# One more folded piece, of 16 rows, at the end of pass one, and other DMA times in the planner of pass two

## The chip, the cores and the metric

The kernel runs on one core of a Trainium2 chip. The metric is the device time of the whole program in microseconds, from several runs; beside it stands one execution taken by the hardware profiler. The engines are called PE (matrix), DVE (vector), ACT (scalar), POOL and SP (here it only issues the DMAs of rows).

## The reference

The input `x` is 1 x 384 x 384 x 384 in bfloat16, the weight `w1d` one number (k = 1, so the padding is empty):

```python
g = jnp.einsum("bhwc->bc", x) / (H * W)
s = jnp.zeros_like(g)
for i in range(k):
    s = s + gp[:, i:i + C] * w1d[i]
s = _sigmoid(s)
return x * s[:, None, None, :]
```

So each channel's mean over all 147,456 positions is needed before the first output can be written. `x` has 113 MB and does not fit on chip; it is read once for the mean, and what was not kept is read a second time for the product.

## The kernel before

**Rows.** The positions are dealt to 128 partitions, 1152 to each. A "row" below is one position in every partition: 384 channels, 768 B a partition, 98,304 B in all. A chunk of n rows in one DMA is a run of n x 768 B in each partition. The tile `arena` holds `ROWS` rows; all loads, scales and stores work in it.

**Pass one** sums the rows: every row that lands is multiplied on PE with a matrix of ones (`sum_rows`, L253, one matmul a row, all into one PSUM bank). Rows of the first chunk (`STREAMED`, 785 rows) are summed and overwritten; rows of the second (`KEPT`, 367 rows) stay. To keep more rows than there is room for, groups of rows are **folded** (`fold`, L292): of a piece of p = 4 rows times four (16 rows), the exponent bits that all values share are taken out, so that the fourth row of each four is hidden in bits of the other three; 16 rows then take 12. `GROUPS` lists the groups: the first piece (16 rows), eight pairs of pieces (32 rows each) in two columns, and `BANKED`, whose folded rows are parked in PSUM. A fold is 10 instructions on DVE and 2 tests on ACT (L313) that check that the bits are as assumed; it uses 16 scratch rows, T (8 rows) and Y (8 rows). The loop at L416 takes each group (`take`), folds it and streams other rows meanwhile through the room not used yet (`BETWEEN`, `SLOTS` of 13 rows from A). At the end `take_raw` (L433) fills all that is left, the scratch last, with kept rows that are not folded: U, V (8 rows each), the 39 rows from A, Y and T. The seam follows: last matmul, sigmoid into `s_bf` (L443), a copy of it in PSUM (L447).

**Order in pass one.** All row DMAs are issued by SP in the order of the program, and each first waits for the last reader of the rows it overwrites (PE's sum, DVE's or ACT's last use). So a load that waits holds back all loads behind it.

**Pass two** scales and stores the kept rows, unfolds the groups (`unfold`, L470: DVE steps `fields`, `three`, `fourth`, which rebuild and scale three quarters and then the last quarter of a piece), and reads the 785 streamed rows again through whatever room has come free, scales and stores them. POOL scales three pieces of 4 rows beside DVE. The order of SP's and DVE's instructions is not written by hand: a **planner** (L564 to L767) steps a clock in 0.05 us, with a cost per row (`ROW`), per load and store, a latency before a transfer moves (`LAT`) and until its end is seen (`SEEN`), and emits each load, scale, unfold step and store when its model says that it is due. `needed` holds the scratch rows that must be stored before a column of groups may be unfolded, `home` and `free` say which column a group uses, `order` in which order the groups come. The planner fixes the order alone; on the chip each instruction still waits for its semaphores.

Of the kernel before, what the change touches and what calls it, by code (L numbers as in the profile page):

```python
# [127 lines left out]
def kernel(  # L128
# [25 lines left out]
    PIECE = 4  # L154
    PAIR = 2 * PIECE
    PAIRS = 4
    U = 3 * PIECE + PAIRS * 3 * PAIR
    G0 = U + PAIR
    V = G0 + PAIRS * 3 * PAIR
    A = V + PAIR  # L160
    N_A = 39
    T = A + N_A
    Y = T + 2 * PIECE
    ROWS = Y + 2 * PIECE
# [3 lines left out]
    GROUPS = [(0, PIECE)]  # L168
# [4 lines left out]
            GROUPS.append((a + 3 * PAIR * i, PAIR))  # L173
    BANKED = len(GROUPS)
    GROUPS.append((A, 6))
    PS = 3 * GROUPS[BANKED][1]
    N_RAW = ROWS - V + PAIR
    pool = ctx.enter_context(tc.tile_pool(name="sb", bufs=1))
    psum = ctx.enter_context(tc.tile_pool(name="psum", bufs=1, space=bass.MemoryType.PSUM))

# [24 lines left out]
    def rows(lo, n):  # L205
        return [("a", r) for r in range(lo, lo + n)]
# [5 lines left out]
    N_STREAM = RPP - N_RAW - sum(4 * q for _, q in GROUPS)  # L212
    N_KEPT = RPP - N_STREAM
    assert N_STREAM % 2 and N_KEPT % 2
    STREAMED, KEPT = (0, N_STREAM), (N_STREAM, N_KEPT)
    r = 0
    c_group = []
# [3 lines left out]
    c_raw = r  # L221
    assert r + N_RAW == N_KEPT

    def raw(a):

        return c_raw + (a - U if a < G0 else PAIR + a - V)


    summed = [0]
# [43 lines left out]
    def bits(dst, src, op0, s0, op1, s1, reads, writes):  # L273
        fl.add(
            "DVE",
            lambda: nc.vector.tensor_scalar(out=dst, in0=src, scalar1=s0, scalar2=s1, op0=op0, op1=op1),  # L276
            reads=reads, writes=writes,
        )

    def join(dst, a, b, op, reads, writes):  # L280
        fl.add(
            "DVE", lambda: nc.vector.tensor_tensor(out=dst, in0=a, in1=b, op=op), reads=reads, writes=writes  # L282
        )

    def flat(a, p):
        return arena[:, a : a + p, :].bitcast(u16)

    SHL, SHR, AND, OR, XOR = (
        Op.logical_shift_left, Op.logical_shift_right, Op.bitwise_and, Op.bitwise_or, Op.bitwise_xor,
    )  # L290
# [56 lines left out]
    streamed = [0]  # L347
# [10 lines left out]
    def stream_all(where, n=None):  # L358
        i = 0
        n = sum(m for _, m in where) if n is None else n  # L360
        while n:
            a, m = where[i % len(where)]
            m = min(n, m)
            stream(m, a)
            n -= m
            i += 1

    def take(g, lo=0, hi=None):

        a, q = GROUPS[g]  # L370
        hi = 4 * q if hi is None else hi
        load(KEPT, a + lo, c_group[g] + lo, c_group[g] + hi)
        sum_rows(a + lo, hi - lo)

    def of_group(g):
        return [i for i, piece in enumerate(pieces) if piece[0] == g]
# [12 lines left out]
    for i, bk in enumerate(banks):  # L389
# [4 lines left out]
    S1, S2, S3 = ([slot] for slot in SLOTS)  # L394
# [8 lines left out]
    BETWEEN = [  # L403
        LOW_COLUMN, HIGH,
        LOW_COLUMN, [(A, 39)],
        [(G0 - 24, 24), (A - 24, 24)], (S1, S2 + S3),
        (S1, S2 + S3 + S1), (S2, S3 + S1),
    ]
    between = sum(n for b in BETWEEN for w in b for _, n in (w if isinstance(w, list) else [w]))
    first = N_STREAM - between  # L410
    stream_all(EARLY[3:], first % 48)
    stream_all(EARLY, first - first % 48)
# [3 lines left out]
    for g, where in zip(range(1, BANKED), BETWEEN):  # L416
# [6 lines left out]
        else:  # L423
# [4 lines left out]
            take(g, 12, 24)  # L428
            fold(k2)
            stream_all(where[1])  # L430
    assert streamed[0] == N_STREAM

    def take_raw(a, n):  # L433
        load(KEPT, a, raw(a), raw(a) + n)
        sum_rows(a, n)

    for a, n in S2 + [(U, 8)] + S3 + S1 + [(V, 8), (Y + 2, 6), (T + 6, 4), (T + 3, 3), (T + 1, 2), (T, 1)]:
        take_raw(a, n)
    assert summed[0] == RPP

# [29 lines left out]
    def unfold(k, first):  # L470

        g, lo, p = pieces[k]
        a, at = first + 3 * lo, first + 3 * GROUPS[g][1] + lo
        w, wc = flat(a, 3 * p), [rows(a + j * p, p) for j in range(3)]
        w0, w1, w2 = (flat(a + j * p, p) for j in range(3))
        ba, ca = Y, Y + PIECE
        u, b, c = flat(at, p), flat(ba, p), flat(ca, p)
        uc, bc, cc = rows(at, p), rows(ba, p), rows(ca, p)

        def fields():  # L480
            bits(u, w0, SHR, 4, AND, 0x0780, wc[0], uc)
            bits(b, w1, SHR, 8, AND, 0x0078, wc[1], bc)
            bits(c, w2, SHR, 12, AND, 0x0007, wc[2], cc)
            join(u, u, b, OR, uc + bc, uc)
            bits(b, w2, SHL, 4, AND, 0x8000, wc[2], bc)
            join(u, u, c, OR, uc + cc, uc)

        def three():
            wall = wc[0] + wc[1] + wc[2]
            bits(w, w, AND, 0x87FF, OR, 0x3800, wall, wall)  # L490
            join(u, u, b, OR, uc + bc, uc)
            scale(a, 3 * p)

        def fourth():

            bits(u, u, XOR, FIX, AND, 0xFFFF, uc, uc)
            scale(at, p)

        return [
            (fields, 4 * TS(p) + 2 * TT(p)),  # L500
            (three, TS(3 * p) + TT(p) + TT(3 * p)),
            (fourth, TS(p) + TT(p)),
        ]

    def TS(n):
        return 0.15 + 0.1 * n

    def TT(n):
        return 0.15 + 0.2 * n
# [51 lines left out]
    written = []  # L561


    ROW, PER_LOAD, PER_STORE = 0.2267, 0.112, 0.061  # L564
    LAT, SEEN, DT = 2.0, 1.5, 0.05
    PENDING, MERGE = 24.0, 12.0
    BIG, CAP, PART, LOW, LAST = 32, 48, 16, 9.0, 4.0
    DEEP, SHORT = 6.5, 1.0
# [26 lines left out]
    def send(chunk, a, lo, hi, then, known=None):  # L595

        waiting.append((dve_at, hi - lo, then, chunk, a, lo, [] if known is None else known))
# [8 lines left out]


    SCRATCH = rows(Y, 8)
    needed = [set(SCRATCH + rows(U, 8)), set(SCRATCH + rows(V, 8)), set(SCRATCH)]

    def stored(a, n):

        def f():
            for i in range(a, a + n):
                for left in needed:
                    left.discard(("a", i))
                if not Y <= i < Y + 8 and not U <= i < U + 8 and not V <= i < V + 8:
                    idle[i] = True
        return f


    for a, n in (
        (Y, 4), (Y + 4, 4), (T, 4), (T + 4, 4), (A + 26, 6), (A + 32, 7), (A + 13, 13), (V + 4, 4), (A, 13)
    ):
        landed.append((KEPT, a, raw(a), n, True))

# [2 lines left out]
    t = 1.0  # L629
# [3 lines left out]
        alongside.append((t, KEPT, a, raw(a), n))  # L633


    order = [g for i in (3, 2) for g in (1 + 2 * i, 2 + 2 * i)] + [BANKED]
    order += [g for i in (1, 0) for g in (1 + 2 * i, 2 + 2 * i)] + [FIRST]
    line = deque(order)
    home = {g: i for i, column in enumerate(COLUMNS) for g in column}
    home[BANKED] = 2  # L640
    free = [True, True, True]
    total = len(GROUPS)
    out_rows = 0
    turns = deque()
# [5 lines left out]
    def start_group():  # L650

        if not line:
            return False
        g = line[0]
        column = home[g]
        if needed[column] or not free[column] or g == BANKED and (bank_at is None or now < bank_at[1]):
            return False
        line.popleft()
        free[column] = False
        a, q = GROUPS[g]  # L660
        if g == BANKED:
            a = bank_at[0]

        below = 0
        if column < 2 and g != COLUMNS[column][0]:
            below = GROUPS[COLUMNS[column][COLUMNS[column].index(g) - 1]][1]

        def part():
            release(a + below, sent - below)

        def done():
            nonlocal out_rows
            out_rows += 1
            free[column] = True
            release(a + max(below, sent), 4 * q - max(below, sent))

        for k in of_group(g):
            fields, three, fourth = unfold(k, a)
            turns.extend((fields + (None,), three + (None,), fourth + (None,)))
        sent = 0  # L680
        if len(line) >= total - N_SPLIT and q == PAIR:

            f, t, _ = turns[-5]
            sent = 3 * PIECE
            turns[-5] = (f, t, lambda: send(KEPT, a, c_group[g], c_group[g] + sent, part, written))
        f, t, _ = turns[-1]
        turns[-1] = (f, t, lambda: send(KEPT, a + sent, c_group[g] + sent, c_group[g] + 4 * q, done, written))
        return True

    while True:  # L690

        if dve_at <= now:
# [4 lines left out]
            if landed and (ahead < PENDING or not can):  # L697
                chunk, a, lo, n, end = landed.popleft()
# [43 lines left out]
        if got and todo < N_STREAM:  # L742
            n, a = max(got)
            n = min(n, CAP, N_STREAM - todo)
            ahead = backlog()

            queue = sum(e[1] for e in moves)
            turn = last_is_load or queue >= DEEP or queue < SHORT
            if turn and (todo or not landed and not waiting) and (n >= BIG or n == N_STREAM - todo or (ahead < LOW and n >= 8) or ahead < LAST):
                last_is_load = True  # L750
                load(STREAMED, a, todo, todo + n)
                for i in range(a, a + n):
                    idle[i] = False
                parts = [(STREAMED, a + e, todo + e, f - e, f == n) for e, f in split(n, PART)]
                todo += n
                moves.append([now + LAT, n * ROW + PER_LOAD, lambda parts=parts: landed.extend(parts)])
# [44 lines left out]
```

## Time and profile before

| what | value |
|---|---|
| median of 3 runs | 720.13 us (719.99 to 720.31) |
| the profiled execution, its own time | 720.71 us |
| its span, first to last instruction | 718.7 us |
| busy: DVE, PE, ACT, POOL | 494.5, 211.0, 115.7, 9.8 us |
| DMA | 303.79 MB, mean 423 GB/s |
| HBM read, written | 190.41 MB, 113.25 MB |
| last matmul of pass one ends, first store is issued | 267.80, 269.42 us |

The span is cut in 40 slices of 18 us in the page's second part; a digit is a unit's busy share in tenths. A row of the chain of waits has a start, a length and what was waited for; start plus length of a DMA row is the moment at which that transfer had landed. In a timeline row stand start, length, engine, line, operation, shapes and count.

### The profile page before, as it was taken

How to read it: one execution, taken by the hardware profiler on the slowest of the kernel's cores; microseconds unless marked ns; L12 is line 12 of the kernel's file. 1: busy time of each engine (PE TensorE's matmuls, PEld its weight loads, DVE VectorE, ACT ScalarE, POOL GpSimd, SP SyncE). 2: the span in 40 equal slices, each digit the busy share in tenths (PEclk: the TensorE clock that was granted, in tenths of full speed). 3: DMA queues.
4: the chain of work that ended last, by engine and by line, in shares of the span. 5: the costliest groups of instructions: out<-in, count | busy, mean ns of one | idle time of the engine just before them, and what ended most of it. 6: DMA issues, size and time to landing. Idle time of an engine off the chain costs nothing.

```text
span 718.7 us, 2062 instructions
## 1 busy us (share of the span) xinstructions
PE 211.0 (29%) x1202; PEld 0.3 (0%) x3; DVE 494.5 (69%) x472; ACT 115.7 (16%) x93; POOL 9.8 (1%) x7
## 2 busy tenths in 40 slices
PE   4678778987887770000000000000000000000000
PEld 0000000000000000000000000000000000000000
DVE  4600003888999719998999999999999865450840
ACT  3600002666677510002000000000000000000000
POOL 0000000000000004000000000000000000000000
PEclk9899999999999995555555555555555555555555
DMA  9999999999999979999999999999999999999997
GB/s 383 428 444 429 427 427 437 436 437 422 427 426 428 428 330 392 405 429 427 428 429 424 431 436 433 431 438 429 437 429 433 428 435 430 439 429 429 434 437 307
DMA packets 20173, 303.79 MB, mean 423 GB/s; under 512 B 2242, under 2 KB 2498, under 8 KB 5570
## 3 DMA queue, kind: packets, MB, share of 16 engines
q1 hardware_dynamic: 20160, 303.67, 99.0%
q8 instruction: 4, 0.07, 0.0%
q14 instruction: 7, 0.06, 0.0%
q10 hardware_dynamic: 2, 0.00, 0.0%
HBM read 190.41 MB, written 113.25 MB: 422 GB/s over the span
## 4 chain that ended last, share of the span: by engine, by line
DMA 72%; DVE 16%; PE 5%; ACT 2%; another core or an unknown queue 1%; SPq 0%; issue 0%; DVEq 0%
DMA arena<-in_x_dram 54%; DMA out_dram<-arena 19%; DVE arena L456 12%; PE bank L242 5%; DVE arena L276 3%; ACT arena L313 2%; DVE arena L282 1%; SPq L236 0%; ACT s_bf L443 0%; SPq L466 0%; DVEq L112 0%; SPq L796 0%; SPq L112 0%; SPq L106 0%
## 5 line engine op out<-in xcount | busy, mean ns | idle before, releaser
L456 DVE TENSOR_TENSOR arena<-arena,s_bf 128x1536 bf16<-128x1536 bf16 (+9 forms) x97 | 229.0, 2390 | 76.0 <-DMA arena<-in_x_dram 60.3
L276 DVE TENSOR_SCALAR arena<-arena 128x1536 uint16<-128x1536 uint16 (+2 forms) x247 | 145.3, 633 | 118.1 <-DMA arena<-in_x_dram 102.1
L242 PE MATMUL bank<-arena,ones 128*128 128x384 bf16 x1151 | 202.5, 336 | 48.2 <-DMA arena<-in_x_dram 48.0
L313 ACT ACTIVATE arena<-arena 128x3072 uint16<-128x3072 uint16 (+1 forms) x38 | 102.5, 2696 | 142.1 <-DVE arena L276 142.1
L282 DVE TENSOR_TENSOR arena<-arena 128x1536 uint16<-128x1536 uint16 (+2 forms) x114 | 121.0, 1061 | 5.0 <-PE bank L242 2.6
L529 PE MATMUL bank<-odd,ones 128*128 128x1 bf16 x1 | 0.2, 187 | 322.7 <-DVE odd L524 322.7
L456 POOL TENSOR_TENSOR arena<-arena,s_bf 128x1536 bf16<-128x1536 bf16 x3 | 9.6, 3238 | 268.4 <-ACT bank L447 268.4
L386 ACT COPY arena<-bank 128x512 uint32<-128x512 uint32 (+1 forms) x7 | 4.0, 571 | 56.2 <-DMA out_dram<-arena 56.0
L456 DVE TENSOR_TENSOR arena<-arena,bank 128x1536 bf16<-128x1536 bf16 (+3 forms) x8 | 11.6, 1520 | 0.0
L242 PE MATMUL bank<-zeros,ones 128*128 128x384 bf16 x48 | 8.3, 326 | 0.0
L313 ACT ACTIVATION_READ_ACCUMULATOR arena<-arena 128x1 f32 x38 | 7.1, 186 | 0.0
L386 ACT COPY bank<-arena 128x512 uint32<-128x512 uint32 (+1 forms) x7 | 3.6, 567 | 0.0
L443 ACT ACTIVATE s_bf<-bank,w_sc 128x384 bf16<-128x384 f32 x1 | 0.6, 581 | 14.2 <-PE bank L242 14.2
L256 PE MATMUL bank<-arena,ones 128*128 128x384 bf16 x1 | 0.5, 478 | 6.7 <-DMA arena<-in_x_dram 6.7
L769 ACT ACT_TABLE_LOAD x1 | 1.3, 1283 | 0.7 <-PEq L785 0.7
L343 DVE TENSOR_SCALAR w_sc<-bank 128x1 f32<-128x1 f32 x1 | 0.2, 159 | 1.1 <-PE bank L338 1.1
L333 DVE MEMSET ones<- 128x128 bf16 x1 | 0.2, 165 | 1.1 <-SPq L106 1.1
L338 PE MATMUL bank<-w_bf,ones 1*128 1x1 bf16 x1 | 0.2, 182 | 2.1 <-DMA w_bf<-in_w1d_dram 2.1
L529 PEld LDWEIGHTS bank<-odd,ones 128*128 128x128 bf16 x1 | 0.1, 105 | 581.4 <-DVE odd L524 581.4
L533 DVE CAST odd_i<-bank 128x1 int32<-128x1 f32 x1 | 0.2, 159 | 0.3 <-PE bank L529 0.3
L447 ACT COPY bank<-s_bf 128x192 uint32<-128x192 uint32 x1 | 0.3, 323 | 0.0
L519 DVE TENSOR_REDUCE worst<-seen 128x1 f32<-128x38 f32 x1 | 0.2, 186 | 0.0
(8 smaller groups left out, 0.9 us busy)
## 6 DMA issues: line engine op xcount, KB each, us to landing
arena<-in_x_dram SPq DMA_DIRECT2D x15, 4608.0 KB, 35.5
arena<-in_x_dram SPq DMA_DIRECT2D x20, 1248.0 KB, 14.2
out_dram<-arena SPq DMA_DIRECT2D x6, 3072.0 KB, 33.0
out_dram<-arena SPq DMA_DIRECT2D x4, 4608.0 KB, 40.2
arena<-in_x_dram SPq DMA_DIRECT2D x5, 3072.0 KB, 22.5
arena<-in_x_dram SPq DMA_DIRECT2D x6, 2304.0 KB, 18.5
out_dram<-arena SPq DMA_DIRECT2D x11, 1248.0 KB, 10.9
arena<-in_x_dram SPq DMA_DIRECT2D x3, 4512.0 KB, 27.2
```

Source lines behind the costliest of these rows:

```text
L242: return pe.add_instruction(mybir.InstMatmult(name=nc.get_next_instruction_name(), ins=[pe.lower_ap(rhs), pe.lower_ap(ones[:])], outs=[pe. ...
L256: return nc.tensor.matmul(acc, lhsT=ones[:], rhs=arena[:, i, :], start=first, stop=last)
L276: lambda: nc.vector.tensor_scalar(out=dst, in0=src, scalar1=s0, scalar2=s1, op0=op0, op1=op1),
L282: "DVE", lambda: nc.vector.tensor_tensor(out=dst, in0=a, in1=b, op=op), reads=reads, writes=writes
L313: lambda: nc.scalar.activation(out=y, in_=y, func=ACTF.Copy, accum_out=seen[:, 2 * k + i : 2 * k + i + 1]),
L333: fl.add("DVE", lambda: nc.vector.memset(ones[:], 1.0), writes=["ones"])
L386: "ACT", lambda: nc.scalar.copy(dst.bitcast(u32), src.bitcast(u32)), reads=reads, writes=writes
L443: lambda: nc.scalar.activation(out=s_bf[:], in_=acc, func=ACTF.Sigmoid, scale=w_sc[:, 0:1]),
L447: "ACT", lambda: nc.scalar.copy(s_ps.bitcast(u32), s_bf[:].bitcast(u32)), reads=["s_bf"], writes=["bank0"]
L456: lambda: vec.tensor_tensor(out=v, in0=v, in1=s[:, None, :].to_broadcast([P, n, C]), op=Op.mult),
L529: lambda: nc.tensor.matmul(votes, lhsT=ones[:], rhs=odd[:], start=True, stop=True),
L769: nc.scalar.preload_act_table(ACTF.Sigmoid)
```

## The change

- A new group `LATE` of one piece (16 rows) lies at A, where slots lay before. It is taken and folded after the eight pairs. Its 12 folded rows stay from A, and `D` = A + 12 names the 4 rows that come free; the rows kept raw go from 71 to 59, so 371 rows are kept instead of 367 and 781 are streamed.
- The slots of the last two pairs and the final raw loads are cut anew: 13, then 16 and 10 rows; 8 streamed rows (`SPARE`) go through U while the new piece is folded.
- In pass two `LATE` is unfolded first, in a home of its own (3), which waits until Y and D are stored.
- `unfold` has four steps instead of three: `fields` is cut in `fields` and `signs`, with the same six instructions in another order.
- The planner's `LAT` goes from 2.0 to 0.4 us.

```diff
+    LATE = len(GROUPS)
+    GROUPS.append((A, PIECE))
+    D = A + 3 * PIECE
     PS = 3 * GROUPS[BANKED][1]
-    N_RAW = ROWS - V + PAIR
+    N_RAW = 2 * PAIR + ROWS - D
...
-        return c_raw + (a - U if a < G0 else PAIR + a - V)
+        return c_raw + (a - U if a < G0 else PAIR + a - V if a < A else 2 * PAIR + a - D)
...
         [(G0 - 24, 24), (A - 24, 24)], (S1, S2 + S3),
-        (S1, S2 + S3 + S1), (S2, S3 + S1),
+        (S1, S2 + S3), ([(A, 16)], [(A + 16, 10)] + S3),
     ]
+    SPARE = [(U, 8)]
...
+    take(LATE)
+    for k in of_group(LATE):
+        fold(k)
+    stream_all(SPARE)
+    assert streamed[0] == N_STREAM
+
-    for a, n in S2 + [(U, 8)] + S3 + S1 + [(V, 8), (Y + 2, 6), (T + 6, 4), (T + 3, 3), (T + 1, 2), (T, 1)]:
+    for a, n in [(D + PIECE, 10)] + S3 + [(V, 8), (U, 8), (D, PIECE), (Y + 2, 6), (T + 6, 4), (T + 3, 3), (T + 1, 2), (T, 1)]:
         take_raw(a, n)
...
             bits(b, w1, SHR, 8, AND, 0x0078, wc[1], bc)
+            join(u, u, b, OR, uc + bc, uc)
+
+        def signs():
             bits(c, w2, SHR, 12, AND, 0x0007, wc[2], cc)
-            join(u, u, b, OR, uc + bc, uc)
             bits(b, w2, SHL, 4, AND, 0x8000, wc[2], bc)
             join(u, u, c, OR, uc + cc, uc)
...
-            (fields, 4 * TS(p) + 2 * TT(p)),
+            (fields, 2 * TS(p) + TT(p)),
+            (signs, 2 * TS(p) + TT(p)),
...
-    LAT, SEEN, DT = 2.0, 1.5, 0.05
+    LAT, SEEN, DT = 0.4, 1.5, 0.05
...
-    needed = [set(SCRATCH + rows(U, 8)), set(SCRATCH + rows(V, 8)), set(SCRATCH)]
+    needed = [set(SCRATCH + rows(U, 8)), set(SCRATCH + rows(V, 8)), set(SCRATCH), set(SCRATCH + rows(D, PIECE))]
...
-        (Y, 4), (Y + 4, 4), (T, 4), (T + 4, 4), (A + 26, 6), (A + 32, 7), (A + 13, 13), (V + 4, 4), (A, 13)
+        (Y, 4), (Y + 4, 4), (D, PIECE), (T, 4), (T + 4, 4), (A + 26, 6), (A + 32, 7), (V + 4, 4), (D + PIECE, 10)
...
-    order = [g for i in (3, 2) for g in (1 + 2 * i, 2 + 2 * i)] + [BANKED]
+    order = [LATE] + [g for i in (3, 2) for g in (1 + 2 * i, 2 + 2 * i)] + [BANKED]
...
-    home[BANKED] = 2
-    free = [True, True, True]
+    home[BANKED], home[LATE] = 2, 3
+    free = [True] * 4
```

More of the change, by code (lines that the diff above doesn't have):

```diff
@@ L406 @@
         [(G0 - 24, 24), (A - 24, 24)], (S1, S2 + S3),
-        (S1, S2 + S3 + S1), (S2, S3 + S1),
+        (S1, S2 + S3), ([(A, 16)], [(A + 16, 10)] + S3),
     ]
-    between = sum(n for b in BETWEEN for w in b for _, n in (w if isinstance(w, list) else [w]))
+    SPARE = [(U, 8)]
+    between = sum(n for b in BETWEEN + [SPARE] for w in b for _, n in (w if isinstance(w, list) else [w]))
     first = N_STREAM - between
@@ L430 @@
             stream_all(where[1])
-    assert streamed[0] == N_STREAM
     def take_raw(a, n):
@@ L608 @@
     SCRATCH = rows(Y, 8)
-    needed = [set(SCRATCH + rows(U, 8)), set(SCRATCH + rows(V, 8)), set(SCRATCH)]
+    needed = [set(SCRATCH + rows(U, 8)), set(SCRATCH + rows(V, 8)), set(SCRATCH), set(SCRATCH + rows(D, PIECE))]
+    FOURTH = set(rows(U, 8) + rows(V, 8) + rows(D, PIECE) + SCRATCH)
     def stored(a, n):
@@ L616, in f @@
                     left.discard(("a", i))
-                if not Y <= i < Y + 8 and not U <= i < U + 8 and not V <= i < V + 8:
+                if ("a", i) not in FOURTH:
                     idle[i] = True
@@ L677, in start_group @@
         for k in of_group(g):
-            fields, three, fourth = unfold(k, a)
-            turns.extend((fields + (None,), three + (None,), fourth + (None,)))
+            turns.extend(step + (None,) for step in unfold(k, a))
         sent = 0
         if len(line) >= total - N_SPLIT and q == PAIR:
-            f, t, _ = turns[-5]
+            f, t, _ = turns[-6]
             sent = 3 * PIECE
-            turns[-5] = (f, t, lambda: send(KEPT, a, c_group[g], c_group[g] + sent, part, written))
+            turns[-6] = (f, t, lambda: send(KEPT, a, c_group[g], c_group[g] + sent, part, written))
         f, t, _ = turns[-1]
```

## The prediction

> **What bounds the kernel now.** I read the slices of the span first, because they show at once which unit is never idle.
>
> ```profile
> DMA  9999999999999979999999999999999999999997
> GB/s 383 428 444 429 427 427 437 436 437 422 427 426 428 428 330 392 405 429 427 428 429 424 431 436 433 431 438 429 437 429 433 428 435 430 439 429 429 434 437 307
> ```
>
> The 16 DMA engines are busy in every slice but the one at the seam of the two passes and the last one, so the time is the number of rows moved times the time of a row, plus the places where the queue is not at full rate. The chain of waits says the same:
>
> ```profile
> DMA 72%; DVE 16%; PE 5%; ACT 2%; another core or an unknown queue 1%; SPq 0%; issue 0%; DVEq 0%
> ```
>
> Then the stretches, to see at which rate and where it dips (columns: engines' busy time, PE clock, DMA share, GB/s).
>
> ```profile
> 64.00:135.00 71.00, 58.85 (x338) 0.00 (x0) 14.80 (x20) 11.43 (x8) 0.00 (x0) 0.95 1.01 435
> 136.00:250.00 114.00, 93.69 (x557) 0.00 (x0) 100.13 (x135) 77.14 (x54) 0.00 (x0) 1.00 1.01 430
> 300.00:420.00 120.00, 0.00 (x0) 0.00 (x0) 113.56 (x96) 4.00 (x7) 0.00 (x0) 0.50 1.01 429
> 260.00:270.00 10.00, 7.08 (x43) 0.00 (x0) 1.57 (x2) 0.90 (x2) 1.17 (x1) 1.00 0.58 234
> 270.00:280.00 10.00, 0.00 (x0) 0.00 (x0) 10.00 (x8) 0.00 (x0) 8.46 (x3) 0.58 1.01 412
> 280.00:290.00 10.00, 0.00 (x0) 0.00 (x0) 9.93 (x12) 0.00 (x0) 0.00 (x0) 0.50 1.03 401
> 290.00:300.00 10.00, 0.00 (x0) 0.00 (x0) 9.97 (x10) 0.00 (x0) 0.00 (x0) 0.50 0.99 386
> ```
>
> A row (128 partitions of 768 B, 98,304 B) costs 98,304 B / 435 GB/s = 0.226 us where transfers are 32 to 48 rows long. Three things lie above that rate: the seam near 267 us, a slow patch from 270 to 300 us, and small transfers (430 and 429 GB/s). DVE is busy 113.56 of 120 us from 300 to 420, so it hides behind the DMA with little room.
>
> **The change part by part.**
>
> 1. *Rows.* The kept rows go from 367 to 371, so the rows read twice go from 785 to 781. Four rows fewer at 0.226 us: **-0.90 us**. All of it is on the bound, the DMA queue.
>
> 2. *Transfers.* I counted SP's list in both kernels: 140 row transfers before (51 in pass one, 89 in pass two), 152 after (52 and 100). Slots of 13 rows became 16 and 10, and pieces of 24 or 32 rows became more and smaller ones. What one more transfer costs inside a full queue comes from two places. In the chain of waits these two landings
>
> ```profile
> 236.84 13.94 DMA arena<-in_x_dram
> 253.13 8.44 DMA arena<-in_x_dram
> ```
>
> are at 250.78 and 261.57, and SP's list has 13, 8, 13 and 13 rows between them: 10.79 us for 47 rows in 4 transfers. 47 x 0.226 is 10.62, so 0.04 us a transfer. The stretch 300 to 420, at 429 instead of 435 GB/s, loses 1.4% of 120 us, 1.7 us, on about 32 transfers: 0.05. I take 0.04, the lower, because it is free of the planner's other waits: 12 x 0.04 = **+0.48 us**; the bounds are 0 and 0.05 (0 to +0.6). SP issues the twelve in 0.34 us each, while it mostly waits.
>
> A store with nothing ahead of it shows what the queue hides:
>
> ```profile
> out_dram<-arena SPq DMA_DIRECT2D x1, 384.0 KB, 2.3
> ```
>
> That is the first store, issued at 269.42; 4 rows carry 0.94 us of that, so 1.4 us are fixed. Such a cost is met only where the queue is empty. The Trainium skill ("DMA: Bandwidth & Descriptors", Measured) says to batch to at least 1 MiB for 75% of peak, and (Anatomy of one DMA) puts a fixed 2.0 us on each; it speaks against this change, whose 10-row pieces are 960 KB. By that rule the twelve transfers would cost 24 us. Here four transfers averaging 1.1 MB took 10.79 us, 428 GB/s, so queued transfers do not show it in this trace.
>
> 3. *One fold more at the end of pass one.* Consecutive folds of one piece start 7.83 us apart:
>
> ```profile
> 219.16 1.90 DVE L276 TENSOR_SCALAR arena<-arena 128x3072 uint16<-128x3072 uint16 x3
> 226.99 1.90 DVE L276 TENSOR_SCALAR arena<-arena 128x3072 uint16<-128x3072 uint16 x3
> 253.47 0.19 ACT L313 ACTIVATION_READ_ACCUMULATOR arena<-arena 128x1 f32 x1
> ```
>
> It costs nothing as long as the loads queued behind it come early enough. Before, the last load landed near 267.2 us (issued near 255.9, 11.4 to landing). Counting back from there over the new list (1, 2, 3, 4, 6 rows, then D 4, U 8, V 8, S3 13, 10, spare 8; 0.226 a row, 0.04 a transfer), the new piece's 16 rows land at 251.7. DVE is free by then: the last pair's first 12 rows arrive some 3 us sooner, since a 13-row load ahead of them is gone and with it the 2.6 us that DVE waited for them at 237; its two folds run from 234.8 to 250.6. So the new fold runs from 251.7 to 259.5. The 6-row load into the scratch waits for the last ACT test, which ended 7.80 us after its fold's start before (253.66 against 245.86): it is issued at 259.6, and the queue has work until 263.4. That is 3.8 us of cover; the first load of the program, 24 rows or 5.4 us landing 7.9 us after issue, shows a start-up of 2.5. **0 us, with 1.3 us to spare**; beyond that each us of a later fold is a us of time. The seam itself (last matmul, sigmoid, first scale, first store) is not edited: 0.
>
> 4. *The opening of pass two.* DVE unfolds the new piece first and stores its 16 rows in one go. Order on the queue: stores of 59 rows in 12 transfers, loads of 21 and 10 rows, then this store. From 270.8 (first data) that is 59 x 0.226 + 0.48 = 13.8 us to 284.6, and 7.1 us more to 291.7. DVE's side: eight scales of 47 rows, 12.47 us before for nine scales of 59 rows less 12 x 0.2 us and one start, so 268.43 to 278.4. Then one unfold, from the pitch of
>
> ```profile
> 280.82 1.49 DVE L276 TENSOR_SCALAR arena<-arena 128x1536 uint16<-128x1536 uint16 x3
> 290.62 1.49 DVE L276 TENSOR_SCALAR arena<-arena 128x1536 uint16<-128x1536 uint16 x3
> ```
>
> 9.8 us, so the store goes out at 288.3: 3.4 us of cover, less 1.4 fixed, **2.0 us to spare** (before, the first unfolded store went out at 289.3 with work until 301.4). The next three stores (10, 11, 10 rows, scales of 2.15, 2.35, 2.15 us after the loads land at 289.4 and 291.7) go out at 291.6, 294.0 and 296.1 and are needed at 295.4, 297.7 and 300.2; then 47 rows of loads need no DVE and the cover grows to some 9 us. I carried the same running sum on, DVE's durations against rows: the thinnest place further on is near 360 us, some 3 us. So 0; the piece adds 6.4 us of conversion to DVE (9.8 less the scales 2.47 and 0.96), hidden by DMA.
>
> 5. *The planner's latency, the split of the unfold into four steps, the fourth home.* They change only the order that is counted in 2 and 4. SP, POOL (its three scales are the same) and ACT get no work on the path: 0.
>
> Sum: -0.90 + 0.48 = -0.42 us. The profiled execution took 720.71 us (span 718.7 and 2.0 around it), so 720.29 by its own measure; it stands 0.58 above the median of the runs, 720.13, and against that the forecast is **719.7 us**. About 0.2%, 1.44 us, is what a measurement of this kernel can tell from no change; this is inside.
>
> **The rivals.**
>
> *The slow patch moves (faster).* From 270 to 300 the rates are 412, 401 and 386 with the DMA share at 0.99 to 1.03: the engines are busy and slow, no wait explains it. Against 430 this is 10 us x (0.042 + 0.067 + 0.102) = 2.1 us. The change replaces just these transfers (13-row stores and loads by 10). If the patch goes, 719.7 - 2.1 = 717.6; half of it, 718.7. For it: the rate is 429 once the order settles. Against: the new opening is the same kind, small stores and then the first loads. It could as well double: 721.8.
>
> *The queue runs dry where the new piece is stored (slower).* Place: the 16-row store of part 4. It decides when DVE is over 2.0 us later than 288.3. Were its 6.4 us of conversion to take double time, the price would be 6.4 - 2.0 = 4.4 us; were DVE 4.5 us late, 2.5, which I take as the middle of what can happen: 719.7 + 2.5 = **722.2 us**. For it: 12 us of cover shrink to 3.4, and DVE is at 9.9 of 10 us there. Against: DVE's unfold took the same 9.8 us at 280 and at 333, however busy the queue.
>
> *Every added transfer shows its fixed part (slower).* 12 x 1.4 - 0.90 = +15.9, 736 us, from the first store's row above. The 47 rows in 10.79 us speak against it. (It is the mechanism behind the rule of the Trainium skill's page "DMA: Bandwidth & Descriptors", Anatomy of one DMA.)
>
> **How the numbers follow.** Forecast (within 0.2%) 0.56; patch mostly gone 0.28; queue dry 0.10, patch worse 0.05, fixed costs 0.01. So faster 0.28, same 0.56, slower 0.16. The range goes from the patch all gone (717.6, with a little for the transfers' cost at nothing) to the patch doubled or the queue dry by 2 us: **717.3 to 721.8**; the forecast alone has 719.2 to 719.8 from the bounds in part 2.
>
> **What would show it.** HBM read should be 190.02 MB (190.41 less four rows). The last matmul of pass one should end near 267.8; if the DMA share dips between 255 and 264, part 3 is wrong. The window 280 to 300 should have a DMA share near 1; a dip near 292 is the dry queue, a rate of 425 or more the moved patch. From 300 on the rate should stay at 428 to 433. A rate visibly below that would mean that the smaller transfers cost more than 0.04 us.

## The result and the profile after

The changed kernel took **722.52 us** (median of 9 runs, 721.27 to 724.43), the kernel before 720.17 in the runs beside it (719.82 to 720.95, 9 runs): ratio 1.0033, 95% interval 1.0024 to 1.0042. So it is 2.35 us slower; forecast was 719.7, with a range that ended at 721.8.

First the page of the profiled execution (722.54 us, span 720.8), the lines that answer to those of before:

```profile
DMA  9999999999999989999999999999999999999997
GB/s 384 418 445 438 426 426 435 437 433 429 424 426 427 423 321 394 406 418 414 422 435 423 436 427 430 437 424 431 425 443 428 433 436 436 425 432 435 436 425 299
...
HBM read 190.02 MB, written 113.25 MB: 421 GB/s over the span
...
DMA 62%; DVE 22%; ACT 8%; PE 5%; issue 0%; SPq 0%
```

The DMA engines are as busy as before, and the bytes are those that were forecast (190.02 MB). The chain names more DVE and ACT, since the load into the scratch now waits for the new fold and the chain runs back from there through the folds, but the DMA row is at 9 in the same slices, so the bound is still the queue. What fell is the rate in the 18th to 20th slice, 306 to 360 us: 418, 414, 422 where it was 429, 427, 428. No wait shows there; the engines are busy and slow. The stretches say the same (columns: length, PE, PE loads, DVE, ACT, POOL busy, PE clock, DMA share, GB/s):

```profile
250.00:260.00 10.00, 7.33 (x44) 0.00 (x0) 9.07 (x12) 7.47 (x6) 0.00 (x0) 1.00 1.00 422
260.00:270.00 10.00, 7.39 (x44) 0.00 (x0) 1.05 (x2) 0.90 (x2) 0.65 (x1) 1.00 0.68 251
270.00:280.00 10.00, 0.00 (x0) 0.00 (x0) 9.97 (x11) 0.00 (x0) 8.98 (x3) 0.57 0.94 381
280.00:290.00 10.00, 0.00 (x0) 0.00 (x0) 8.80 (x9) 0.00 (x0) 0.00 (x0) 0.50 1.04 404
290.00:300.00 10.00, 0.00 (x0) 0.00 (x0) 8.91 (x8) 0.00 (x0) 0.00 (x0) 0.50 0.99 380
300.00:420.00 120.00, 0.00 (x0) 0.00 (x0) 112.37 (x98) 4.00 (x7) 0.00 (x0) 0.50 1.01 425
420.00:700.00 280.00, 0.18 (x1) 0.10 (x1) 215.38 (x165) 0.00 (x0) 0.00 (x0) 0.50 1.00 432
```

From 300 to 420 the rate is 425 where it was 429: 120 x 4/429 = 1.1 us. From 420 to 700 it is 432 where it was 433, which is little more than rounding. At the seam, 260 to 270, the engines are busy for 0.68 of the time (0.58 before): the last load lands some 0.6 us later, and the first store starts as much later, which is the 0.94 and 381 of the next row (1.01 and 412 before). This does not come with every execution: in e1, the same kernel again, the last load lands where it did before.

The landings of the transfers, one after another, give the sum. What lies above 0.2265 us a row and 0.04 us a transfer comes to 8.3 us in the whole of before and 10.6 in after, 2.3 more; 0.6 of that is at the seam and 1.9 between 305 and 370, and the other stages come to -0.2 (the opening of pass two up to 305 has 1.0 less, the part behind 420 has 0.9 more). Less the forecast's 0.42 that is 1.9, and the last transfer lands at 718.85 us instead of 716.93.

The loss has places. Two shorter stretches of before,

```profile
310.00:320.00 10.00, 0.00 (x0) 0.00 (x0) 9.96 (x11) 0.00 (x0) 0.00 (x0) 0.50 1.03 434
330.00:345.00 15.00, 0.00 (x0) 0.00 (x0) 14.66 (x17) 0.00 (x0) 0.00 (x0) 0.50 1.01 426
```

and the same of after:

```profile
310.00:320.00 10.00, 0.00 (x0) 0.00 (x0) 9.96 (x7) 0.00 (x0) 0.00 (x0) 0.50 1.02 418
330.00:345.00 15.00, 0.00 (x0) 0.00 (x0) 13.52 (x10) 1.76 (x3) 0.00 (x0) 0.50 1.01 412
```

In the trace's packets these are stretches of 1 to 3 us: near 314 us some packets of 7,680 B take up to 700 ns where 291 is the median, near 336 some of 8,448 B take up to 975 where it is 319. Below they are called slow places. Both kernels have two in the opening of pass two (before near 287 and 298, after near 285 and 292); those past 300 us are what after has in addition, and these two fall on the last load ahead of a store.

### The profile page after: what moved, and what is told of

Its sections match the earlier page's. It is cut to its first block, busy times and chain, and to the rows that moved or that the text cites. A ratio compares the mean times of both kernels' runs of the same rounds, so it can differ in the third digit from the quotient of the medians.

```text
span 720.8 us, 2101 instructions
## 1 busy us (share of the span) xinstructions
PE 213.5 (30%) x1202; PEld 0.3 (0%) x3; DVE 508.8 (71%) x494; ACT 121.4 (17%) x97; POOL 9.8 (1%) x7
## 3 DMA queue, kind: packets, MB, share of 16 engines
HBM read 190.02 MB, written 113.25 MB: 421 GB/s over the span
## 4 chain that ended last, share of the span: by engine, by line
DMA 62%; DVE 22%; ACT 8%; PE 5%; issue 0%; SPq 0%
DMA arena<-in_x_dram 43%; DMA out_dram<-arena 18%; DVE arena L465 14%; ACT arena L316 8%; DVE arena L279 6%; PE bank L245 5%; DVE arena L285 2%; SPq L239 0%; ACT s_bf L452 0%; SPq L807 0%; SPq L106 0%
## 5 line engine op out<-in xcount | busy, mean ns | idle before, releaser
L465 DVE TENSOR_TENSOR arena<-arena,s_bf 128x4608 bf16<-128x4608 bf16 (+7 forms) x100 | 231.7, 2348 | 82.0 <-DMA arena<-in_x_dram 71.9
L279 DVE TENSOR_SCALAR arena<-arena 128x1536 uint16<-128x1536 uint16 (+3 forms) x260 | 153.0, 634 | 105.6 <-DMA arena<-in_x_dram 98.3
L245 PE MATMUL bank<-arena,ones 128*128 128x384 bf16 x1151 | 205.1, 340 | 46.1 <-DMA arena<-in_x_dram 45.8
L285 DVE TENSOR_TENSOR arena<-arena 128x1536 uint16<-128x1536 uint16 (+2 forms) x120 | 127.8, 1065 | 7.6 <-PE bank L245 4.4
L316 ACT ACTIVATE arena<-arena 128x3072 uint16<-128x3072 uint16 (+1 forms) x40 | 108.0, 2699 | 142.3 <-DVE arena L279 142.3
L465 DVE TENSOR_TENSOR arena<-arena,bank 128x1536 bf16<-128x1536 bf16 (+3 forms) x8 | 9.2, 1221 | 0.0
L259 PE MATMUL bank<-arena,ones 128*128 128x384 bf16 x1 | 0.5, 479 | 6.7 <-DMA arena<-in_x_dram 6.7
```

The source lines that it names most:

```text
L245: return pe.add_instruction(mybir.InstMatmult(name=nc.get_next_instruction_name(), ins=[pe.lower_ap(rhs), pe.lower_ap(ones[:])], outs=[pe. ...
L259: return nc.tensor.matmul(acc, lhsT=ones[:], rhs=arena[:, i, :], start=first, stop=last)
L316: lambda: nc.scalar.activation(out=y, in_=y, func=ACTF.Copy, accum_out=seen[:, 2 * k + i : 2 * k + i + 1]),
L465: lambda: vec.tensor_tensor(out=v, in0=v, in1=s[:, None, :].to_broadcast([P, n, C]), op=Op.mult),
```

## Experiments

Each was measured beside the kernel before on the same chip; ratios are to that.

**e1 and e2: both kernels again**, unchanged.

> The changed kernel once more, for a second profile. Three explanations of the 2.3 us that it lost are open. Order: the slow places of the DMA (near 264, 285, 292, and the last loads of a group at 314, 337, 365 us) belong to the order and size of the transfers; they return at the same transfers, within some tenths of a us. Chance: the same amount, about 4 us of slow packets, at other places. Addresses in HBM: the same places too, so this run alone does not tell it from order. Time 722.5, 721.3 to 724.4.

> The kernel before once more. Order or addresses: slow places again at the end of the last store ahead of the first load of pass two (286 to 289 us) and in the 13-row load after it (296 to 299), and nearly none from 305 to 370. Chance: they lie elsewhere, and 305 to 370 may be hit. Time 720.2.

After 722.08 us (ratio 1.0024, 1.0013 to 1.0034), before 720.53 (1.0006, 0.9996 to 1.0016). The slow places of after came back at 292, 314 and 336 us, with one near 395 that had been faint in the first profile (packets of 18,432 B up to 1,826 ns now, 882 then, where 686 is the median), and before had none of that size past 300: they belong to the program and are no accident of one execution.

**e3: after without the bit conversions of pass two.**

```diff
         def fields():
-            bits(u, w0, SHR, 4, AND, 0x0780, wc[0], uc)
...
+            pass
         def signs():
...
+            pass
```

> The changed kernel without the bit conversions of pass two (the folded rows are scaled and stored as they are, so these outputs hold other values); every transfer and its order stay. DVE has some 122 us less to do in pass two. Contention of DVE with the DMA in SBUF: the slow places from 283 to 370 us mostly go, the stretch 300 to 420 rises from 425 to 430 GB/s or more, and the time falls by 2 to 4 us, to about 719. Order or addresses: the slow places stay and the time stays within 0.7 us of 722.5, since the queue is not dry. Dry queue: it falls too, but then the DMA share of some window had been under 0.95.

721.81 us (1.0024, 1.0012 to 1.0037), with slow places past 300 still there and 423 GB/s from 300 to 420. (The outputs of the folded rows hold other values here, as in e9.) DVE's added conversions are not the cause.

**e4: the kept chunk ahead of the streamed one in HBM.**

```diff
-    STREAMED, KEPT = (0, N_STREAM), (N_STREAM, N_KEPT)
+    KEPT, STREAMED = (0, N_KEPT), (N_KEPT, N_STREAM)
```

> The changed kernel with the kept chunk first in HBM and the streamed chunk behind it; the order, the sizes and the places in SBUF stay. Addresses: the slow places move or go and the time changes by 1 us or more either way. Order, contention: same places and a time within 0.7 us of 722.5.

721.66 us (1.0015, 1.0005 to 1.0025), the same places: not where the chunks begin. (It leaves the number of rows in each chunk as it is. That was overlooked until e12.)

**e5: before with its stores of 24 rows and more cut in two**, 23 transfers more.

```diff
     def store(chunk, a, lo, hi):
+        if hi - lo >= 24:
+            mid = lo + (hi - lo) // 2
+            written.append(store(chunk, a, lo, mid))
+            a, lo = a + mid - lo, mid
```

> The kernel before, with each of its 23 stores of 24 rows or more issued as two halves, one behind the other; nothing else moves: 163 transfers instead of 140. Number: every transfer more costs what the change's twelve seem to have cost, (2.2 + 0.9) / 12 = 0.26 us, so the time rises by 6 us, to 726. Order (slow places bound to where a group of loads or stores ends, small transfers cheap): 23 x 0.04 = 0.9 us, so 721.2, and the places at 286 and 297 us are the same as before.

The edit cuts 19 stores and not 23: the four of 48 rows fall into three pieces, since the first half, of 24 rows, is cut again. The transfers are 163, as expected.

721.91 us (1.0019, 1.0009 to 1.0028): 1.45 us over the 720.46 beside it, 0.06 us a transfer. The number of transfers costs about what was forecast.

**e6 to e8: other orders of the planner for after**: the unfold in three steps as before (e6), `LAT` at 1.0 (e7) and at 2.0 (e8).

```diff
-            (fields, 2 * TS(p) + TT(p)),
-            (signs, 2 * TS(p) + TT(p)),
+            (fields, 4 * TS(p) + 2 * TT(p)),
...
-    LAT, SEEN, DT = 0.4, 1.5, 0.05
+    LAT, SEEN, DT = 1.0, 1.5, 0.05
```

> The changed kernel with the unfold in three steps as before: the planner gives another order, 148 transfers instead of 152. Number: 4 x 0.26, 1 us less, 721.2. Order: the slow places at 285 and 292 us stay (the opening is the same), those after 310 lie elsewhere, and the time is anything between 720 and 723.

> The changed kernel with the planner's latency at 1.0: 150 transfers in another order, the running sum finds no dry queue (thinnest cover 1.6 us beyond the fixed part). Number: 0.5 us less than the changed kernel, 721.8. Order: other slow places after 310 us, 720 to 723.

> The changed kernel with the planner's latency at 2.0 as before the change: 150 transfers, but the running sum of DVE against the queue finds two places where the store of unfolded rows comes late, 0.2 us near 294 and 1.3 us near 316. So 1.5 us more than the changed kernel with no other slow place, about 723.8, and a window near 316 with a DMA share under 0.95. If the time is the same or less, the sum's cover is too pessimistic or the slow places weigh more than a dry queue.

e6 722.04 us (1.0021, 1.0010 to 1.0033), e7 723.95 (1.0042, 1.0028 to 1.0056), e8 722.42 (1.0031, 1.0018 to 1.0043). Where the slow places lie goes with the order; that there are some past 300 us does not. e7 is a miss: it came out above both of its numbers (721.8, and 720 to 723), and its rate from 300 to 420 is 419 GB/s, the lowest of all; why it loses more is not known. The dry queue that was expected of e8 near 316 us did not come. Its stretch

```profile
310.00:320.00 10.00, 0.00 (x0) 0.00 (x0) 10.00 (x5) 0.00 (x0) 0.00 (x0) 0.50 1.02 421
```

has no idle DMA. That slow loads gave DVE the time it lacked is argued from this and was not tried.

**e9: after with DVE almost idle in pass two**: e3, and each DVE scale does only its first row.

```diff
-        v = arena[:, a : a + n, :]
+        m = 1 if eng == "DVE" else n
+        v = arena[:, a : a + m, :]
```

> The changed kernel without the bit conversions of pass two and with each DVE scale done on the first row of its chunk alone (the other rows are stored as they were read, so the outputs hold other values); transfers, their order and their waits stay. DVE then has some 20 us of work in pass two instead of 315. If anything that DVE does in SBUF slows the DMA, the slow places at 285, 292, 314, 336 and 395 us go and the time falls below 720. If they belong to the order of the transfers alone, they stay at the same transfers and the time stays within 1 us of 722.2.

721.75 us (1.0012, 1.0002 to 1.0021). The stretch from 300 to 420:

```profile
300.00:420.00 120.00, 0.00 (x0) 0.00 (x0) 10.03 (x32) 3.99 (x7) 0.00 (x0) 0.50 1.01 425
```

DVE works 10.03 of 120 us instead of 112, and the rate is still 425. Neither DVE's time nor its traffic in the arena slows the DMA.

**e10: before with the loads of up to 26 rows in pass two cut in two** (20 transfers more).

```diff
+        if streamed[0] == N_STREAM and chunk == STREAMED and hi - lo <= 26:
+            mid = (lo + hi) // 2
+            load_one(chunk, a, lo, mid)
+            a, lo = a + mid - lo, mid
```

> The kernel before, with its 20 loads of pass two of up to 26 rows issued as two halves each (5 to 13 rows); order and waits stay, 160 transfers instead of 140. If small loads ahead of a store are what makes the slow places, as the changed kernel's 10- and 11-row loads suggest, this gets more of them: over 3 us slower, 723.5 or more, with the stretch 300 to 420 under 425 GB/s. If a transfer costs 0.04 to 0.06 us wherever it stands, 0.8 to 1.2 us: 721.1 to 721.6.

721.52 us (1.0011, 1.0001 to 1.0021): 0.97 over the 720.55 beside it, 0.05 a transfer. From 300 to 420:

```profile
300.00:420.00 120.00, 0.00 (x0) 0.00 (x0) 115.05 (x97) 4.00 (x7) 0.00 (x0) 0.50 1.02 428
```

Loads of 5 to 13 rows do not bring the rate to 425. Small transfers are not the cause.

**e11: after's planner with larger transfers** (`MERGE` 12 to 3; 142 transfers).

```diff
-    PENDING, MERGE = 24.0, 12.0
+    PENDING, MERGE = 24.0, 3.0
```

> The changed kernel with the planner's MERGE at 3 instead of 12, so that a load's parts are stored in one go: 142 transfers instead of 152, loads and stores of 21 rows where there were 10 and 11. By rows and transfers alone it should be 0.9 - 2 x 0.04 = 0.8 us under the kernel before, 719.5. If smaller pieces cause the slow places, it has fewer and comes out under 721; if the places belong to the rest of the order, it stays at 722. The running sum finds a store without spare time near 330 us, up to 1 us.

722.97 us (1.0041, 1.0026 to 1.0056). A miss: ten transfers fewer gave nothing, and the slow places stayed.

**e12 to e15: the distance between partitions.** A chunk of n rows lies in HBM partition by partition, so n x 768 B is the step from one partition to the next. The change turns the two chunks from 785 and 367 rows into 781 and 371, and the step with them. These kernels give the first chunk some rows more and leave the rest as it is: after at 785, 789 and 793, and before at 793.

```diff
-    STREAMED, KEPT = (0, N_STREAM), (N_STREAM, N_KEPT)
+    EXTRA = 4
+    STREAMED, KEPT = (0, N_STREAM + EXTRA), (N_STREAM + EXTRA, N_KEPT - EXTRA)
...
+    def where_in(chunk, lo, hi):
+        if chunk == KEPT and hi > N_KEPT - EXTRA:
+            move = N_STREAM - (N_KEPT - EXTRA)
+            return STREAMED, lo + move, hi + move
+        return chunk, lo, hi
```

> The changed kernel, its 152 transfers in the same order and sizes, with the rows of a partition in HBM dealt as before the change: 785 rows a partition in the first chunk (781 streamed and the 4 kept rows of D) and 367 in the second. Pitch: the slow places after 310 us go as in the kernel before, and the time is rows and transfers alone, 720.4 - 0.9 + 0.6 = 720.1, at most 720.5. Order: they stay, 722.

> The same with 789 and 363 rows (the 8 kept rows of U lie in the first chunk). Pitch: the slow places change with the distance, the time is over 0.7 us away from 722.2, either way. Order: 722, same places.

> The same with 793 and 359 rows (U and D in the first chunk). Pitch: another time again, over 0.7 us away from 722.2 or from the run with 789. Order: 722, same places.

> The kernel before, in its own order, with 793 and 359 rows (U in the first chunk) instead of 785 and 367. Pitch: slow places move, a time over 0.7 us away from 720.4. Order: 720.4, slow places at 287 and 297 us alone.

After at 785 took 721.52 us (1.0009, 0.9998 to 1.0020), at 789 721.46 (1.0017, 1.0006 to 1.0028), at 793 721.53 (1.0014, 1.0004 to 1.0025); before at 793 720.87 (1.0002, 0.9992 to 1.0012). By the times, e13 alone agrees with what was written for the distance. e12 was to take at most 720.5, e14 a time of its own and e15 one over 0.7 us from 720.4, and none did: 785, 789 and 793 rows give about the same time. How far these lie from 781 the times did not settle, since after itself had not run on that chip. The stretch from 300 to 420 says more. This is e12:

```profile
300.00:420.00 120.00, 0.00 (x0) 0.00 (x0) 112.96 (x100) 3.99 (x7) 0.00 (x0) 0.50 1.01 428
```

and e13 and e14 have 429 and 428 there: after's order, its small transfers and its DVE work at before's rate.

**e16 to e18: the square closed on one chip.** Before's order at after's distance (781 and 371; three transfers are cut in two, one near 250 us and two at the very end, where no slow place is), after's order at before's distance once more, and after itself.

```diff
-    STREAMED, KEPT = (0, N_STREAM), (N_STREAM, N_KEPT)
+    LESS = 4
+    STREAMED, KEPT = (0, N_STREAM - LESS), (N_STREAM - LESS, N_KEPT + LESS)
...
+        if chunk == STREAMED and lo < STREAMED[1] < hi:
+            load(chunk, a, lo, STREAMED[1])
+            a, lo = a + STREAMED[1] - lo, STREAMED[1]
```

> Before, with the partitions of HBM as far apart as in after (781 rows in the first chunk, 371 in the second); the last four streamed rows lie in the second chunk, so one load in pass one and one load and one store in pass two are cut in two (3 more transfers, 0.15 us by 0.05 each). If the distance between partitions makes after slow: about 1 us more than before, 721.5, and slow places in 305 to 400. If it is the order of the transfers alone: 720.3 to 720.8, and slow places only near 287 and 298, as in before.

> After's order once more with before's distance (785 and 367 rows), now beside after itself on one chip. If the distance is part of it: 0.6 to 1 us below the run of after beside it, and less than 0.8 us of excess in 305 to 370. If the earlier 721.5 was scatter: within 0.4 us of after.

> After unchanged, as the measure for the other two. 722.1 to 722.5 by all theories, slow places at 292, 314, 336 and 395.

| us, median (ratio to before, 95% interval) | 785 and 367 rows | 781 and 371 rows |
|---|---|---|
| before's order | 720.67 (kernel before) | 722.71 (1.0034, 1.0022 to 1.0046) |
| after's order | 720.63 (0.9998, 0.9989 to 1.0007) | 722.31 (1.0026, 1.0016 to 1.0036) |

The columns differ by 2.04 and 1.68 us; 2.04 less three transfers at 0.05 is 1.9. That is the way that was expected of the distance and more than was expected (721.5 for e16; 0.6 to 1 us for e17 below e18). The rows of the table differ by no more than 0.4. The kernel of before, with nothing of the change but the four rows' place in HBM, is as slow as after. Its page, e16:

```profile
GB/s 382 433 437 428 426 428 433 437 435 428 425 426 429 427 318 409 404 414 422 416 423 430 431 431 439 424 441 424 440 427 437 423 434 442 428 432 438 436 427 301
```

and that of e17, after's order at before's distance:

```profile
GB/s 385 421 448 433 429 427 436 436 434 422 424 428 427 428 327 394 407 425 428 426 436 418 431 428 435 433 430 437 422 451 430 433 428 436 423 446 427 441 416 291
```

Read the 18th to 20th number: 414, 422, 416 against 425, 428, 426. The dip of after is in e16, without a new fold, a new piece or a new order, and it is gone from e17, which has all of them. The slow places follow in the main: in e16 they fall on loads of before's own order (near 317, 328 and 372 us). In e17 the one at 336 is gone, but the last loads near 344 and 395 us stay slow, the latter in e12 and e14 too, so the distance does not make all of them. By the landings the excess between 305 and 370 is 2.8 us in e16 and 0.4 and 1.0 in the two profiles of before, 2.5 in e18 and 1.2 in e17, where under 0.8 was expected. So in before's order the whole loss is there; in after's order it is 1.3 us, and e18 has 0.8 more at the seam, which the distance may not have caused (see the fold below). The stretches of 120 us, e16 first, then e17 and e18:

```profile
300.00:420.00 120.00, 0.00 (x0) 0.00 (x0) 111.37 (x95) 4.00 (x7) 0.00 (x0) 0.50 1.01 424
```

```profile
300.00:420.00 120.00, 0.00 (x0) 0.00 (x0) 112.54 (x98) 4.00 (x7) 0.00 (x0) 0.50 1.01 428
```

```profile
300.00:420.00 120.00, 0.00 (x0) 0.00 (x0) 111.40 (x98) 4.00 (x7) 0.00 (x0) 0.50 1.01 425
```

Over all profiles the row separates without an overlap: at 781 rows (after, e1, e3, e4, e6 to e9, e11, e16, e18) it is 419 to 426, whatever the order; at 785, 789 and 793 (before, e2, e5, e10, e12 to e15, e17) it is 428 to 430.

What stays open: why 781 rows are slow and three other counts are not, and whether the streamed chunk (781) or the kept one (371) does it, since the two always changed together. Pass one reads the same chunks without the dip (the 11th to 13th slice is 425, 426, 429 in e16 and 424, 428, 427 in e17), so the distance alone is not enough; that the alternation of loads and stores has to come to it is argued from this and was not tried by itself. From 420 to 700 us, where larger transfers alternate as well, the rate is 432 GB/s in e16 and 433 in before, so their size may have a part in it too. Open too is the order's own worth: e12 and e17 are one and the same kernel, 0.9 us over before on one chip and level with it on the other. The profiles of e12 and e13 have a late load at the seam and that of e17 has none, which may be a part of it.

## Why the prediction was wrong, point by point

- **Rows, -0.90 us: the step that failed.** It took four rows off the queue at 0.226 us each and left the price of all the others as it was. But the two counts are also the step between partitions, and at the new one the program costs more: 1.9 us in before's order, all of it in pass two, and 1.7 in after's, of which the profiles put 1.3 there (e16 to e18). The saving in bytes is as forecast (190.02 MB). With the distance put back e17 stands at 0.9998 (0.9989 to 1.0007), which holds the forecast's -0.42 us (0.9994). But e12, the same kernel on another chip, stands at 1.0009 (0.9998 to 1.0020), which does not, so only one of the two runs bears out the saving in time. Of the 2.8 us between forecast and result, the distance is 1.7 to 1.9 and the transfers' price 0.1 to 0.2; the rest, 0.7 to 1.0, is not divided further. The prediction's line "from 300 on the rate should stay at 428 to 433" is where it showed: 425.
- **How that line was to be read was wrong too.** A lower rate was to mean that "the smaller transfers cost more than 0.04 us". e10 has 20 more small loads and stays at 428; e16 has three transfers more and falls to 424.
- **Transfers, +0.48 us: about right.** e5 and e10 give 0.06 and 0.05 a transfer (by their intervals 0.03 to 0.09 and 0 to 0.08), so twelve cost 0.6 to 0.7. The rival of the fixed part is out. The Trainium skill ("DMA: Bandwidth & Descriptors", Anatomy of one DMA) puts a fixed 2.0 us on each transfer, and does so for transfers that POOL (GpSimd) issues, which the prediction did not say. Here SP issues them all, and in this full queue the measured 0.05 to 0.06 decides.
- **The fold at the end of pass one, 0 us: the times held.** The load behind the new fold was forecast to be issued at 259.6, the store of the new piece at 288.3. In the chain of waits of after:

```profile
259.62 5.80 DMA arena<-in_x_dram
268.95 10.07 DVE arena L465 x9
288.86 9.31 DMA out_dram<-arena
```

  The first row is that load, at 259.62. The sign that was named against this part, a dip of the DMA share between 255 and 264, did not come; the share is 1.00 and only the rate is lower, 399 GB/s for 420 (before, then after):

```profile
255.00:264.00 9.00, 7.04 (x43) 0.00 (x0) 0.00 (x0) 0.00 (x0) 0.00 (x0) 1.00 1.00 420
255.00:264.00 9.00, 7.59 (x45) 0.00 (x0) 4.34 (x7) 3.50 (x4) 0.00 (x0) 1.00 1.00 399
```

  DVE begins pass two at 268.95, 0.5 later than forecast, because that 6-row load's packets were slow. Of the 14 profiles with this fold, 6 have such a delay of 0.4 to 0.9 us at the seam, at 781, 785 and 789 rows; 8 have none, and none of the 6 with before's order has one. So this term is 0 to 0.9 and not 0, and its cause is open.
- **The opening of pass two, 0 us: right.** The store goes out at 288.86, 0.56 later than forecast, as the seam was (the scales ahead of it are nine, not the eight that were counted, and take 10.07 us for 9.97); the DMA share from 280 to 300 is 1.04 and 0.99. The queue did not run dry there, nor in e8.
- **The slow patch from 270 to 300:** it stayed (404 and 380 GB/s from 280 to 300, before 401 and 386; the 381 from 270 to 280 holds the late seam, and e1, without it, has 406 where before had 412). The rival's mechanism, busy engines at a lower rate, is of the kind that decided, but it was looked for in the patch that was there, by the mix of transfers. The loss came behind it, with the addresses, and its price was not among the rivals. So the range ended 0.7 us short.

## What to carry to other kernels

When a change alters a count, follow it to the access patterns: a number of rows that looks like a quantity can also be a stride, and then it can reprice every transfer and not only those added or removed. When all DMA engines are busy and the rate falls with no wait in sight, cross the addresses with the order of the work early, in a square of four kernels on one chip; here that settled what the runs on order, size and engines could not.

## What the runs showed of the hardware

- A step of 599,808 B between partitions (781 rows) cost 1.9 us against 602,880 B (785 rows) in before's order, and 1.7 in after's, where 1.3 shows in pass two; with 789 and 793 rows the rate from 300 to 420 us was that of 785 (428 to 430 GB/s).
- The loss comes in places of 1 to 3 us in which some packets take two to three times as long as the median (700 ns for 291, 975 for 319), mostly at the last load ahead of a store, and with one order they return at the same transfers. A few such places are there at 785 rows as well (e17: near 344 and 395 us).
- One transfer more in a full queue cost 0.05 to 0.06 us, with loads of 5 to 13 rows (e10) as with stores of 12 and more (e5).
